# A searched instruction order with one load of V, half of the second weight's casts on VectorE, and a last output chunk in two column halves

## The chip, the cores and the metric

The kernel runs on one core of one Trainium2 chip. The metric is the device time of one execution in microseconds (us), median of several runs. The profile's span runs from the first to the last instruction and is 1.7 to 1.8 us shorter than the time of the same run (165.7 against 167.47 for the kernel before). Runs carry a state: a run more than 1.5% above the fastest of the same kernel in the same series is called slow and left out of comparisons. With few runs that label is coarse on one core; where it matters I give the granted clock (the share of TensorE's full clock that the chip allowed, mean over the span) beside it.

Engines: PE is TensorE, PEld its weight loads, DVE is VectorE, ACT is ScalarE, POOL is GpSimd, SP is SyncE, and a q after a name is the engine's instruction queue, where DMA issues are shown.

## The reference, cut to what matters

```python
# attention: gated linear recurrence, batch 4, 8 heads, 768 steps, head size 48
state = alpha[:, :, t, :, None] * state + einsum('bhd,bhe->bhde', k[:, :, t], v[:, :, t])
y[:, :, t] = einsum('bhd,bhde->bhe', q[:, :, t], state)
# mixer on x = y as (4, 768, 384)
u  = x + (x.T @ U @ V).T                   # low rank over the 768 steps: U 768x32, V 32x768
ch = maximum(u @ w_ch1, 0) @ w_ch2         # 384 -> 1536 -> 384
out = u + ch
```

The kernel computes the recurrence in chunks of 128 steps: six chunks for each batch, two at a time, called groups 0, 1 and 2.

## The kernel before

The program describes every operation to a small scheduler, `Plan`, with an engine, an assumed duration, a priority and its inputs. `Plan.run` replays these assumed times, decides in which order each engine gets its instructions, and only then emits them. The chip knows nothing of the assumed times: each engine works through its list in that order, and an instruction whose input is late holds up those behind it.

The places that the change and the argument touch, with cuts:

```python
# V is loaded four times, into four groups of 32 partitions
for g in range(4):
    P.add("POOL", 500, lambda g=g: nc.gpsimd.dma_start(vm_sb[32*g : 32*g+R, :], moe_V), ...)

# the two weights come in three pieces each; every piece is cast to bf16 in two halves
# (i < 3: first weight, i >= 3: second weight)
e = ((("POOL","POOL"),)+(("POOL","POOL"),)*2+(("POOL","POOL"),)*3)[i][hf]
...
op = P.add(e, cost[e], f_cast, r=[(t, i)], w=[...], prio=400 + i, port=True)

# attention, batch 0: which engine makes the products for groups 0, 1, 2
ek = ("DVE", "DVE", "POOL")[g] if first else "POOL"              # k times exp(-cum)
eq = ("DVE", "POOL", "POOL+DVE")[g] if first else (...)           # q times exp(cum)
parts = [(i, 1) for i in range(G)] if first and g in (2,) else [(0, G)]
...
for eng, dst, src, fac in ((ek, rk, kt, ai), (eq, rq, qt, aa)):
    for i0, n in parts if dst is rq else [(0, G)]:
        P.add(e, ..., f_mul(e, dst, src, fac, i0, n), ..., port=True)

# first MLP product: 12 blocks, evicted in turn by ScalarE and VectorE
if jt % 2 == 0:
    P.add("ACT", 500, ... Relu ..., w=[(h1, jt)], prio=100)
else:
    P.add("DVE", 560, ... tensor_scalar_max ..., w=[(h1, jt)], prio=100)

# second MLP product of a chunk: 12 matmuls, one sum on VectorE, one store
P.add("DVE", 550, lambda: nc.vector.tensor_tensor(ou(), xb()[:, c, :], hb()[:, 0, 0:DM], op=ALU.add), ...)
P.add("SP", 550, lambda: nc.sync.dma_start(out[b, c*C:(c+1)*C, :], ou()), ...)
```

The "first stage" below is batch 0's attention, from the start to the first MLP matmul. The "middle" runs from there to the sum of the last chunk but one; the "tail" is the rest.

## Time and profile before

| kernel before | us |
|---|---|
| median of the first three runs (range) | 167.73 (167.64 to 170.92) |
| profile: span | 165.7 |
| first MLP matmul | 31.23 |
| start of the sum of the last chunk but one | 160.37 |

The page's lines and the table of stretches are in the prediction. Two places, of which it has the numbers but not the lines: here they are from the timeline of the kernel before (start, duration, engine, source line, operation, out<-in, count, and in brackets the idle time before it with what ended it). First the first stage:

```profile
15.04 1.64 POOL L448 TENSOR_TENSOR rk<-io,ai 128x768 bf16<-128x768 f32 x1 [5.79 <-ACT ai L441]
...
15.48 2.01 DVE L448 TENSOR_TENSOR rq<-io,aa 128x768 bf16<-128x768 f32 x1
```

VectorE began its product 0.44 us after GpSimd had begun one, and it took about twice as long as one alone (the prediction has the numbers). Then the arrival of the second weight:

```profile
41.65 1.60 POOL L322 CAST w_sb<-io 128x768 bf16<-128x768 f32 x2 [7.65 <-DMA io<-in_moe_w_ch_dram]
```

GpSimd stood 7.65 us before the second weight came in at 41.65. PE had no wait for GpSimd in those 7.65 us, so the wait cost nothing. The stretches around it, from the table by stretch (duration, then busy us and instructions of PE, PEld, DVE, ACT and POOL, granted clock, DMA share, GB/s):

```profile
36.00:40.00 4.00, 3.85 (x38) 2.38 (x37) 1.17 (x3) 3.98 (x7) 0.00 (x0) 1.00 1.07 338
40.00:44.00 4.00, 4.00 (x27) 2.39 (x26) 2.33 (x5) 3.39 (x9) 2.35 (x3) 1.00 1.06 400
44.00:50.00 6.00, 5.38 (x43) 3.25 (x42) 0.96 (x2) 4.69 (x8) 6.00 (x7) 1.00 1.08 326
```

PE works through the arrival at full clock.

### The profile page before, as it was taken

Reading aid. Unit: us, or ns where it says so; the run is one execution under the profiler, and the core shown is the slowest. Engines: PE = TensorE matmul, PEld = TensorE weight load, DVE = VectorE, ACT = ScalarE, POOL = GpSimd, SP = SyncE. Lnnn points to the kernel's source line nnn. Section 1 sums busy time; section 2 is a strip of 40 time slices with the busy share of each in tenths; the row PEclk is TensorE's granted clock in tenths of the full one; section 3 lists DMA queues with packets and bytes.
Section 4 is the critical chain, followed back from the end, with each engine's and each line's share of the span. In section 5 each row is a group of like instructions: output and inputs, shape, how many; then the busy total and the mean of one; then the engine's idle time right before and its main releaser. Section 6 shows DMA issues by size and latency. Waiting matters only on the chain.

```text
span 165.7 us, 3925 instructions
## 1 busy us (share of the span) xinstructions
PE 156.9 (95%) x1635; PEld 96.0 (58%) x1635; DVE 89.9 (54%) x142; ACT 82.5 (50%) x153; POOL 54.0 (33%) x59
## 2 busy tenths in 40 slices
PE   5999999999989999999998899999999999999991
PEld 1454666656556767556556656576656565656560
DVE  2008983553508528588446719996849524544421
ACT  3169277569881894994625575434441212422200
POOL 8923864620994650486002239600000000000000
PEclk9999999999999999999999999999999999999999
DMA  3999999999999999999986998999003713001112
GB/s 99 274 288 203 194 190 384 349 283 368 383 316 316 244 322 249 262 336 313 225 200 137 317 295 113 207 213 171 24 6 82 155 69 120 4 1 68 70 56 95
DMA packets 58851, 33.15 MB, mean 200 GB/s; under 512 B 31440, under 2 KB 57680, under 8 KB 58832
## 3 DMA queue, kind: packets, MB, share of 16 engines
q1 hardware_dynamic: 46992, 24.38, 56.2%
q10 hardware_dynamic: 10864, 8.26, 17.9%
q0 software_dynamic: 976, 0.25, 1.4%
q8 instruction: 13, 0.21, 0.5%
q14 instruction: 6, 0.05, 0.1%
HBM read 24.08 MB, written 4.72 MB: 174 GB/s over the span
## 4 chain that ended last, share of the span: by engine, by line
PE 67%; DMA 10%; SPq 8%; issue 7%; POOL 4%; DVE 1%; ACT 1%; ACTq 0%; POOLq 0%
PE ps L686 28%; PE ps L664 21%; SPq L376 7%; DMA io<-in_moe_w_ch_dram 6%; DMA io<-in_alpha_dram 4%; PE ps L567 2%; PE ps L488 2%; POOL rk L448 2%; PE ps L520 2%; POOL w_sb L322 2%; PE ps L459 2%; PE ps L693 1%; PE ps L633 1%; PE ps L562 1%; POOL io L373 1%
## 5 line engine op out<-in xcount | busy, mean ns | idle before, releaser
L686 PE MATMUL ps<-w_sb,h1t 128*128 128x384 bf16 x288 | 55.3, 326 | 0.0
L664 PE MATMUL ps<-uT,w_sb 128*128 128x384 bf16 x288 | 52.2, 326 | 0.3 <-ACT xb L583 0.3
L675 ACT ACTIVATE h1t<-ps 128x384 bf16<-128x384 f32 x48 | 23.7, 493 | 38.9 <-PE ps L664 38.1
L677 DVE TENSOR_SCALAR h1t<-ps 128x384 bf16<-128x384 f32 x48 | 26.6, 555 | 25.0 <-PE ps L664 22.0
L664 PEld LDWEIGHTS <-w_sb 128*128 128x128 bf16 x288 | 27.7, 98 | 17.9 <-issue 0.5
L686 PEld LDWEIGHTS <-h1t 128*128 128x128 bf16 x288 | 27.3, 98 | 16.9 <-issue 0.5
L498 DVE TENSOR_TENSOR pm<-ps,ut_ones 128x1024 bf16<-128x1024 f32 x18 | 21.5, 1219 | 6.4 <-PE ps L488 3.7
L695 DVE TENSOR_TENSOR ou<-xb,ps 128x384 f32<-128x384 bf16 x24 | 13.2, 552 | 20.9 <-PE ps L693 10.4
L448 POOL TENSOR_TENSOR rk<-io,ai 128x768 bf16<-128x768 f32 x10 | 17.1, 1719 | 18.6 <-ACT ai L441 17.7
L704 PE MATMUL ps<-ones,ident 128*128 128x512 bf16 x55 | 15.4, 422 | 1.9 <-DVE rk L277 1.9
L448 DVE TENSOR_TENSOR rq<-io,aa 128x768 bf16<-128x768 f32 (+1 forms) x11 | 13.1, 1200 | 1.1 <-ACT aa L442 1.1
L322 POOL CAST w_sb<-io 128x768 bf16<-128x768 f32 x12 | 9.5, 828 | 11.4 <-DMA io<-in_moe_w_ch_dram 11.4
L583 ACT CAST xb<-ps 128x768 bf16<-128x768 f32 (+1 forms) x15 | 10.0, 672 | 5.4 <-PE ps L567 4.2
L417 ACT ACTIVATE lt<-io 128x768 bf16<-128x768 f32 x12 | 9.8, 841 | 5.2 <-DMA io<-in_alpha_dram 3.9
L362 POOL TENSOR_SCALAR_AFFINE_SELECT pm<-pm 128x1024 bf16<-128x1024 bf16 x6 | 6.5, 1091 | 17.4 <-DVE pm L498 11.8
L441 ACT ACTIVATE ai<-ps 128x768 bf16<-128x768 f32 x12 | 9.9, 822 | 3.2 <-PE ps L428 1.9
L322 POOL CAST rv<-io 128x768 bf16<-128x768 f32 (+1 forms) x11 | 9.7, 906 | 3.7 <-DMA io<-in_v_dram 3.7
L704 PEld LDWEIGHTS <-ident 128*128 128x128 bf16 x55 | 5.6, 107 | 8.2 <-issue 2.5
L442 ACT ACTIVATE aa<-ps 128x768 bf16<-128x768 f32 x12 | 10.0, 830 | 0.0
L567 PE MATMUL ps<-rv,pm 128*128 128x48 bf16 x192 | 8.3, 184 | 1.2 <-DVE pm L498 1.1
L567 PEld LDWEIGHTS <-pm 128*128 128x128 bf16 x192 | 7.1, 96 | 3.6 <-DVE pm L498 1.6
L505 ACT CAST pm<-ps 128x1024 bf16<-128x1024 f32 x6 | 6.1, 1018 | 5.3 <-PE ps L488 5.3
(66 smaller groups left out, 141.8 us busy)
## 6 DMA issues: line engine op xcount, KB each, us to landing
io<-in_moe_w_ch_dram SPq DMA_DIRECT2D x6, 768.0 KB, 8.9
out_dram<-ou SPq DMA_DIRECT2D x24, 192.0 KB, 2.3
io<-in_q_dram SPq DMA_DIRECT2D x6, 192.0 KB, 4.2
io<-in_v_dram SPq DMA_DIRECT2D x6, 192.0 KB, 4.0
vm_sb<-in_moe_V_dram POOLq DMA_DIRECT2D x4, 48.0 KB, 6.0
kt<-rk SPq DMA_TRANSPOSE x6, 4.0
qt<-rq SPq DMA_TRANSPOSE x6, 3.2
io<-in_alpha_dram SPq DMA_DIRECT2D x4, 0.2 KB, 11.3
```

Of the source, the lines that this page charges most:

```text
L322: ENG[eng].tensor_copy(dst, src)
L376: op = P.add("SP", 950, lambda t=t, src=src, c=c: nc.sync.dma_start(t()[:, :, 0:D].rearrange("p (h c) d -> p c h d", c=NC)[:, c], src[0, : ...
L442: P.add("ACT", 815, lambda: nc.scalar.activation(aa(), cb()[:, :, 0:DM], AF.Exp), r=[cb], w=[aa], prio=pe)
L448: ENG[eng].tensor_tensor(dst()[:, i0 : i0 + n, :, 0:D], ch(src, i0, n), fac()[:, i0 : i0 + n].rearrange("t g (h d) -> t g h d", d=D), op=A ...
L498: nc.vector.tensor_tensor(pmi().rearrange("t two hp c -> t (two hp) c"), sc().rearrange("p two (hp c) -> p (two hp) c", c=C), maskc.to_bro ...
L567: nc.tensor.matmul(y2[:, par, p, :], lhsT=pm[i]()[:, par, p, :], rhs=rv()[:, i, 2 * p + par, :], start=s0, stop=s1, skip_group_check=True,)
L664: nc.tensor.matmul(hb()[:, 0, 0:TW], lhsT=w1_sb[:, ct, jt * 128 : (jt + 1) * 128], rhs=uT()[:, 3 * tt : 3 * tt + 3, ct, :], start=(ct == 0 ...
L675: P.add("ACT", 500, lambda jt=jt, hb=hb: nc.scalar.activation(h1()[:, jt, :], hb()[:, 0, 0:TW], AF.Relu), r=[hb], w=[(h1, jt)], prio=100)
L677: P.add("DVE", 560, lambda jt=jt, hb=hb: nc.vector.tensor_scalar_max(h1()[:, jt, :], hb()[:, 0, 0:TW], 0.0), r=[hb], w=[(h1, jt)], prio=100)
L686: nc.tensor.matmul(hb()[:, 0, 0:DM], lhsT=h1()[:, jt, (c % 3) * C : (c % 3 + 1) * C], rhs=w2_sb[:, jt, :], start=(jt == 0), stop=(jt == NJ ...
L695: P.add("DVE", 550, lambda: nc.vector.tensor_tensor(ou(), xb()[:, c, :], hb()[:, 0, 0:DM], op=ALU.add), r=[hb, (xb, c)], w=[ou], prio=100)
L704: P.fill_fn = lambda i: nc.tensor.matmul(ps[:, i, 0:512], lhsT=ident, rhs=fill_in, start=True, stop=True)
```

## The change

The intent: a new order found by searching over the scheduler's options, with the engines re-assigned to fit; fewer bytes loaded (V once instead of four times, and spread to the four groups of partitions by a matmul); VectorE shares the casts of the second weight, since GpSimd was the busier of the two there; and a shorter end, since the last chunk's sum and store are split in two.

```diff
-        for g in range(4):
-            P.add("POOL", 500, lambda g=g: nc.gpsimd.dma_start(vm_sb[32 * g : 32 * g + R, :], moe_V), ...)
+        P.add("POOL", 500, lambda: nc.gpsimd.dma_start(v16(), moe_V), ...)
+        for hf in range(2):
+            P.add("PE", mm(TW), ... matmul(tb, lhsT=rep4, rhs=v16()[:, hf*TW:(hf+1)*TW]) ...)
+            P.add("DVE", 550, ... copy("DVE", vm_sb[:, hf*TW:(hf+1)*TW], tb) ...)
 ...
-                e = (... +(("POOL","POOL"),)*3)[i][hf]
+                e = (... +(("POOL","DVE"),)*3)[i][hf]
 ...
-        ek = ("DVE", "DVE", "POOL")[g] if first else "POOL"
+        ek = ("DVE", "POOL", "POOL")[g] if first else "POOL"
-        eq = (...) if first else ("DVE" if b in (0,1,2,3) else "POOL")
+        eq = (...) if first else ("DVE" if b in (0,1,2) else "POOL")
-        split = ((1,), (0,), ())[g] if b in (0,1,2) else ()
+        split = ((1,), (0,), ())[g] if b in (0,1) else ()
-        parts = [(i, 1) for i in range(G)] if first and g in (2,) else [(0, G)]
+        parts = [(i, 1) for i in range(G)] if first and g in (0,1,2) else [(0, G)]
 ...  # evictions of kT, qT, v and the state in batch 0, banks, three output buffers for four,
 ...  # store slack 700 for 3000, the scheduler's booking of ScalarE's DMA issues
     def mlp2(b, xb, h1, c, utx):
+        last = b == B - 1 and c == NC - 1
+        for n, (m0, m1) in enumerate(((0, DM // 2), (DM // 2, DM)) if last else ((0, DM),)):
+            ... 12 matmuls, sum and store of columns m0:m1, the same priorities for both halves
```

## The prediction

> **What bounds the kernel now.** I read the page's busy times and slices first, then the chain of waits, then the per-stretch table of busy times, then the timeline at both ends. From the page (busy time, share of span, instructions; then 40 slices of 4.14 us):
>
> ```profile
> PE 156.9 (95%) x1635; PEld 96.0 (58%) x1635; DVE 89.9 (54%) x142; ACT 82.5 (50%) x153; POOL 54.0 (33%) x59
> ...
> PE   5999999999989999999998899999999999999991
> ...
> PEclk9999999999999999999999999999999999999999
> DMA  3999999999999999999986998999003713001112
> ...
> L704 PE MATMUL ps<-ones,ident 128*128 128x512 bf16 x55 | 15.4, 422 | 1.9 <-DVE rk L277 1.9
> ```
>
> PE is the engine to count, but 95% is not all work: line 704 is filler, 55 dummy matmuls that keep the array warm, and a matmul's "busy" includes its pipeline tail. So I counted matmuls by their pitch instead, taken from the merged rows of the chain of waits: 36 of the 384-column matmuls in 5.86 us is 0.163 us each, 8 of the 128-column transposes in 0.45 us is 0.056, 8 or 16 of the small attention ones are 0.020 to 0.028. With the counts of each line that gives about 135 us of real matmul pitch in the whole program, 11.9 us of filler (55 at 0.2155, that is 512/2.4 plus 2.5 ns), and, up to 162.3 us, where the last matmul's result is handed over, about 15 us in which PE has nothing: 1.9 at the start, 5.7 more before 31.2 us, 7.3 after. These pitches are rounded, so each remainder carries perhaps 1 us of error.
>
> The same table of stretches (duration, then busy us of each engine with instruction counts, clock, DMA share, GB/s) shows the three regimes:
>
> ```profile
> 0.00:31.20 31.20, 28.36 (x336) 16.25 (x337) 14.20 (x24) 16.96 (x29) 19.58 (x29) 1.00 0.96 243
> ...
> 45.00:60.00 15.00, 14.51 (x184) 9.83 (x185) 6.50 (x10) 10.05 (x14) 10.12 (x10) 1.00 1.05 294
> 60.00:86.00 26.00, 25.77 (x275) 16.09 (x274) 16.47 (x24) 17.29 (x35) 9.15 (x7) 1.00 1.09 274
> 86.00:97.00 11.00, 9.78 (x196) 6.48 (x195) 6.68 (x8) 5.90 (x11) 2.18 (x2) 1.00 0.90 237
> ...
> 120.00:162.30 42.30, 42.28 (x273) 25.02 (x269) 20.01 (x37) 10.04 (x20) 0.00 (x0) 1.00 0.22 66
> ```
>
> Until 31.2 us the first batch's attention runs behind its loads (DMA share about 1); all filler lies here, the last at 27.5 us, and the first MLP matmul starts at 31.23. From there PE is nearly full; by pitch the holes are about 1.5 us between 31 and 60, about 1 in 60 to 75, 2.4 in 86 to 97, about 1.5 in the rest. From 120 us on there is no hole at all, so nothing that shifts evictions there can help. Then the tail, from the timeline:
>
> ```profile
> 156.27 6.01 PE L686 MATMUL ps<-w_sb,h1t 128*128 128x384 bf16 x36
> ...
> 162.32 0.55 DVE L695 TENSOR_TENSOR ou<-xb,ps 128x384 f32<-128x384 bf16 x1 [1.40 <-PE ps L686]
> ...
> 162.90 0.33 SPq L697 DMA_DIRECT2D out_dram<-ou  x1
> ```
>
> After the last matmul: 0.55 of add, 0.33 of issue, landing 1.9 us after issue start (164.8), end at 165.7: 3.4 us that no PE saving touches. So time = start of MLP (31.2) + remaining pitch (123.8) + holes (7.3) + tail (3.4), and 2.0 us between the span, 165.7, and the median time, 167.73.
>
> **What the Trainium skill says.** "TensorE: Matmul & The Clock Gate", section "Back-to-back issue gap", gives N/2.4 + 2.5 ns: 162.5 ns for 384 columns. The trace agrees (163). For 192 columns that is 82.5 ns, an estimate from the page; weight loads don't bind there as the trace runs 128-column transposes, each with its own load, at 56 ns. "DMA: Bandwidth & Descriptors", section "Anatomy of one DMA", puts most of a small transfer in a fixed part of about 2 us and only the rest in bytes; the last store of 192 KB landed in 1.9 us, with some 0.6 us of engine activity seen, so halving its bytes can save 0.3 us at most. Its section "Issuing engines are not separate DMA queues" says loads from all queues share the 16 engines: so the dropped V loads help only by their bytes. "SBUF — State Buffer" says that VectorE with two SBUF inputs and GpSimd block one another; the trace agrees: a product on VectorE beside a GpSimd product at 15.5 us took 2.01 us, two others, alone, 1.83 together.
>
> **The change, part by part.**
>
> *One V load.* GpSimd issues V four times at 0.50 us each; three go, 1.5 us of GpSimd. But its next task, the copy that gates the q and v loads, then waited 0.41 us for alpha, so issue time is not on the path. 3 x 48 = 144 KB leave saturated engines; at the 225 GB/s of 10 to 20 us that is 0.64 us of transfer, part of it in the shadow of alpha, so the first batch's chunks may land 0.4 us earlier. Added: two matmuls of 384 columns (0.33 us of PE, in time now filled) and two VectorE copies of 0.55.
>
> *First batch's engines.* The second k product moves from VectorE (0.92) to GpSimd (about 1.64), which sat idle 5.8 us until 15.04: VectorE is free 0.9 us earlier. Halving products, casts and evictions by chunk in groups 0 and 1 lets each start when its own chunk lands, at some 0.1 us fixed cost per extra piece. Those pieces and the V copies hand part of the 0.9 back. The end of this stage hangs on the last v chunk (its cast ended at 26.0) and the 5.2 us of state, mask, output, low-rank and eviction after it, which the change hardly shortens. Start of MLP: 0.7 us earlier, 30.5.
>
> *Second weight's casts.* Three of six go from GpSimd (0.83) to VectorE (0.56). In 40 to 50 us GpSimd was busy 8.35 of 10, and PE waited 0.49 us at 46.52 for its k product, which had queued behind two casts. That wait should go: 0.5 us.
>
> *Batches 2 and 3.* For batch 2 the mask loses its ScalarE copy (1.02) plus GpSimd select (1.09) and gets one VectorE product (1.22), two times; these stand in the 86-to-97 hole, where PE waited 1.1 us for a mask and ScalarE lost 0.58 us to issuing a load; the new plan books that issue. Batch 3's q product moves to GpSimd, 3 x 0.95 off VectorE, which is busy 9.4 of 10 between 100 and 110. I give 1.2 of the 2.4. PE work itself is not reduced. Fewer banks for MLP (two kept for attention), the state product confined to two banks, earlier stores with three output buffers instead of four: no net worth I can read, perhaps 0.1 gained.
>
> *The tail.* 12 matmuls at 162.5 become 24 at 82.5: +0.03. Both halves carry the same priorities step by step, and a tie goes to the lower number, so I read the plan as alternating them: half one ends only 0.08 us before half two. Then VectorE does two adds of about 0.35 (the 192-element product at 88.9 took 0.34), the second ending some 0.6 us after the last matmul, against 0.55 before; the issue takes 0.33 and isn't blocked; the last transfer has half the bytes, -0.3. Net -0.25. Had the halves run one after the other it would be about -0.5.
>
> Sum: -0.7 - 0.5 - 1.2 - 0.1 - 0.25 = -2.75, from 167.73: 165.0.
>
> **Rivals.** (1) *The load stream is the bound until about 45 us.* DMA share is about 1 there, GpSimd waited 7.65 us until 41.65 for the second weight, and its loads stay behind the first and alpha. Then an earlier MLP start is given back as a wait for the second weight, and only the transfer saved (0.4), the later holes and the tail count: about 166.0. Against it: after 46 us the casts waited for GpSimd, not for DMA. (2) *VectorE becomes the wait.* It gains 1.1 (V), 1.7 (casts), 2.4 (batch 2 masks) and loses 0.9, 0.7 (one eviction to ScalarE) and 2.9: about +0.8 on 90 busy, so no bound on average; but a late mask or V copy in the first 31 us moves everything, and fewer banks can hold PE back: 167 to 168. (3) *The new order closes nearly all holes.* PE's floor is an MLP start at about 30, 123.8 of pitch, 3.1 of tail and 2.0: 159. With 3 us of holes left: 162. For it: the order was searched with a plan that books more of the hardware's delays. Against: only about half of the holes have a cause that a named edit removes.
>
> **Range and chances.** Middle 165.0; 162.8 if holes fall below 4 us, 167.4 if rival 1 and part of 2 hold. 2% faster is 164.4, a little below my middle: 0.38 for faster, 0.59 for within 2%, 0.03 for slower, as PE work does not grow and the most heavily loaded stretch after 120 us is untouched.
>
> **What would show it.** Right: first MLP matmul near 30.5; no PE wait on a GpSimd product near 46; PE hole in batch 2's attention about halved; the last two adds of 0.35 back to back, and 3.1 to 3.2 us from the last matmul's result to the end. Wrong: the start of MLP unmoved or later (first-batch step), a new PE wait on weight casts after 40 us (rival 1), holes where attention waits for banks or masks (rival 2), or holes after 31 us below 4 us (I was too timid).

## The result

The changed kernel is correct, and slower. In the first series five runs took 172.07, 172.59, 172.69, 172.77 and 176.71 us (the last one slow, at clock 0.961); the kernel before had a median of 167.82. The ratio of the fast runs is 1.0284, 95% interval 1.0253 to 1.0315. Ratios here are the mean time of one kernel's fast runs over the mean of the other's of the same rounds, so not quite the ratio of the medians that I quote. My 165.0 was off by 7.7 us, my range ended at 167.4, and I had given "slower" a chance of 0.03.

The first profile of the changed kernel fell in the slow run, so I don't explain from it. (Its loss looks different: its start is at 37.49 us, and VectorE doesn't wait for the second weight there.) A profile in a fast run came with the repeat called a1 below (time 172.3, granted clock 0.988); its lines answer to those of before. The page:

```profile
span 170.6 us, 3950 instructions
...
PE 159.0 (93%) x1647; PEld 97.4 (57%) x1647; DVE 93.0 (55%) x150; ACT 80.9 (47%) x151; POOL 54.8 (32%) x57
...
PE   5998999982999999999999999999999999999991
...
PEclk9999999999699999999999999999999999999999
```

PE's busy time is only 2 us more than before. The row of slices shows where the time went: a slice is 170.6/40 = 4.27 us, PE falls to 2 in the tenth slice (38.4 to 42.6 us), and the granted clock to 6 in the eleventh. The stretches show it beside the same ones of before:

```profile
36.00:40.00 4.00, 3.07 (x25) 1.75 (x24) 0.21 (x1) 4.00 (x8) 0.00 (x0) 1.00 1.06 322
40.00:44.00 4.00, 1.08 (x6) 0.61 (x6) 1.89 (x4) 0.33 (x2) 2.13 (x2) 0.94 1.05 384
44.00:50.00 6.00, 6.00 (x37) 3.36 (x36) 2.96 (x6) 3.56 (x10) 3.08 (x3) 0.76 0.86 250
```

In 40 to 44 us PE is busy 1.08 us of 4 where before it was busy all 4, and afterwards its clock is 0.76 where before it was 1.00. The timeline there says why:

```profile
41.84 0.56 DVE L328 CAST w_sb<-io 128x768 bf16<-128x768 f32 x1 [5.62 <-DMA io<-in_moe_w_ch_dram]
41.87 1.22 POOL L328 CAST w_sb<-io 128x768 bf16<-128x768 f32 x1 [8.21 <-DMA io<-in_moe_w_ch_dram]
42.31 1.02 DVE L688 TENSOR_SCALAR h1t<-ps 128x384 bf16<-128x384 f32 x2
42.92 2.49 PE L675 MATMUL ps<-uT,w_sb 128*128 128x384 bf16 x9 [3.38 <-DVE h1t L688]
```

Read it from the bottom. PE waited 3.38 us for VectorE's eviction of an MLP block (L688), because the bank that it needed was still full (a bank is one of the eight parts of the tile `ps`, to which PE writes its products). That eviction's own input was long there; it began at 42.31 because it stood behind VectorE's cast of the second weight, and the cast had waited 5.62 us for the weight's load. GpSimd's cast waited 8.21 us for the same load and harmed nobody, exactly as before. So the load's lateness is old (41.65 before, 41.84 now); what is new is that an engine with something urgent behind it waits for it.

To place the rest I use three landmarks of each profile:

| profile | first MLP matmul | middle | tail | span | state of that run |
|---|---|---|---|---|---|
| before | 31.23 | 129.14 | 5.3 | 165.7 | fast |
| changed (a1) | 32.20 | 132.85 | 5.5 | 170.6 | fast |
| difference | +0.97 | +3.71 | +0.2 | +4.9 | |

By an estimate from these lines, the middle's +3.7 fits the hole (3.4) plus the lower clock (0.06 of 4 us and 0.24 of 6 us, 1.7 together), less waits of before that no longer occur, about 1.4 by subtraction.

### The profile page after: what moved, and what is told of

Same layout as the page of the kernel before. It is cut to its first block, busy times and chain, and to the rows that moved or that the text cites. A ratio compares the mean times of both kernels' runs of the same rounds, so it can differ in the third digit from the quotient of the medians.

```text
span 175.0 us, 3950 instructions
## 1 busy us (share of the span) xinstructions
PE 162.5 (93%) x1647; PEld 99.7 (57%) x1647; DVE 93.7 (54%) x150; ACT 81.2 (46%) x151; POOL 54.7 (31%) x57
## 4 chain that ended last, share of the span: by engine, by line
PE 75%; DMA 12%; DVE 5%; POOL 4%; ACT 1%; issue 1%; DVEq 0%; POOLq 0%
PE ps L701 27%; PE ps L675 21%; DMA io<-in_k_dram 12%; PE ps L499 4%; PE ps L470 4%; PE ps L578 4%; PE ps L713 2%; PE ps L573 2%; DVE rq L459 2%; PE ps L531 2%; POOL rk L459 2%; DVE pm L509 1%; PE ps L708 1%; PE ps L644 1%; POOL io L389 1%
## 5 line engine op out<-in xcount | busy, mean ns | idle before, releaser
L701 PE MATMUL ps<-w_sb,h1t 128*128 128x384 bf16 (+1 forms) x300 | 55.4, 320 | 0.0
L688 DVE TENSOR_SCALAR h1t<-ps 128x384 bf16<-128x384 f32 x48 | 26.5, 556 | 30.1 <-PE ps L675 28.0
L459 POOL TENSOR_TENSOR rk<-io,ai 128x768 bf16<-128x768 f32 x11 | 19.1, 1741 | 47.4 <-ACT ai L452 25.7
L509 DVE TENSOR_TENSOR pm<-ps,ut_ones 128x1024 bf16<-128x1024 f32 x20 | 24.2, 1221 | 7.6 <-PE ps L499 6.8
L709 DVE TENSOR_TENSOR ou<-xb,ps 128x384 f32<-128x384 bf16 (+1 forms) x25 | 13.3, 535 | 17.7 <-PE ps L701 9.7
L459 DVE TENSOR_TENSOR rq<-io,aa 128x768 bf16<-128x768 f32 (+1 forms) x9 | 10.9, 1229 | 0.2
L499 PE MATMUL ps<-qt,kt 48*128 48x128 bf16 x192 | 9.0, 232 | 0.4 <-DVE pm L509 0.2
L328 POOL CAST w_sb<-io 128x768 bf16<-128x768 f32 x9 | 7.3, 841 | 5.5 <-DMA io<-in_moe_w_ch_dram 5.5
L326 ACT CAST st<-ps 128x192 bf16<-128x192 f32 x11 | 3.5, 320 | 11.7 <-PE ps L531 7.0
L470 PE MATMUL ps<-ident,rk 128*128 128x128 bf16 x48 | 5.2, 275 | 3.6 <-POOL rk L459 3.3
L326 ACT COPY kt<-ps 128x1024 bf16<-128x1024 bf16 x5 | 5.1, 1026 | 7.4 <-PE ps L470 7.4
```

Of the source, the lines that this page charges most:

```text
L328: ENG[eng].tensor_copy(dst, src)
L459: ENG[eng].tensor_tensor(dst()[:, i0 : i0 + n, :, 0:D], ch(src, i0, n), fac()[:, i0 : i0 + n].rearrange("t g (h d) -> t g h d", d=D), op=A ...
L470: nc.tensor.matmul(t[:, i * HP + p, :], lhsT=src()[:, i, 2 * p : 2 * p + 2, :].rearrange("t h w -> t (h w)"), rhs=ident, start=True, stop= ...
L499: nc.tensor.matmul(s2[:, par, p, :], lhsT=kT()[o : o + D, i, p, :], rhs=qT()[o : o + D, i, p, :], start=(p == 0), stop=(p == HP - 1),)
L509: nc.vector.tensor_tensor(pmi().rearrange("t two hp c -> t (two hp) c"), sc().rearrange("p two (hp c) -> p (two hp) c", c=C), maskc.to_bro ...
L688: P.add("DVE", 560, lambda jt=jt, hb=hb: nc.vector.tensor_scalar_max(h1()[:, jt, :], hb()[:, 0, 0:TW], 0.0), r=[hb], w=[(h1, jt)], prio=100)
```

## The experiments

All kernels below gave correct results. They ran on five chips; each is compared with the kernel before on its own chip. "Start" is the first MLP matmul in the profile.

### First series: is it the first stage?

The slow profile showed the first stage as the late part. Its cause there seemed to be VectorE's products of two SBUF operands beside GpSimd's. So the first theories were about that.

**a0** is the changed kernel again, on another chip.

> The changed kernel once more, to get a profile of an undisturbed run (the one taken first had a granted clock of 0.961 and is not comparable). Time 172.1 to 172.8. Theory of the port: even at a full clock the two half q products of the first group on VectorE take about 2.0 us each (0.55 alone) while GpSimd forms k products, and the first MLP matmul starts 3 to 6 us after the 31.2 us of the kernel before. Rival, the clock: the late start at 37.5 us came from half-speed matmuls between 18 and 29 us; with the clock at 1.0 the start would be within 1 us of 31.2, and the 4.5 us lost would lie after it.

Measured: 173.07, 174.36 and 173.76 us at clocks of 0.979 to 0.985, and 169.93 at 1.00; beside that one the first three count as slow, and no ratio is given. The start was 33.84, 2.6 us later than before's and so a little short of the 3 to 6 expected. This profile fell in one of the slow runs; k1_sp below is the same program in a fast one, and there too the start was 33.70 and the two halves took 3.93 us together. In the first stage (from the timeline of a0):

```profile
13.55 1.79 POOL L459 TENSOR_TENSOR rk<-io,ai 128x768 bf16<-128x768 f32 x1 [4.29 <-ACT ai L452]
...
13.75 2.00 DVE L459 TENSOR_TENSOR rq<-io,aa 128x384 bf16<-128x384 f32 x1
...
15.68 1.99 DVE L459 TENSOR_TENSOR rq<-io,aa 128x384 bf16<-128x384 f32 x1
```

GpSimd's k product began 0.2 us earlier, and each of VectorE's half-size q products, which had been whole in the kernel before, then took 2 us. Half the work, the same 2 us, and each half ends about 0.4 us after a product of GpSimd's (15.75 after 15.34): the time is mostly waiting for GpSimd's instruction to end, and splitting the product made VectorE pay it twice.

**one_q** joins the two halves of group 0's q product again.

```diff
+ if first and g == 0 and dst is rq:        # half 0 does nothing, half 1 does both chunks
+     fm = (lambda *a: None) if i0 == 0 else (lambda e, dst, src, fac, i0, n: f_mul(e, dst, src, fac, 0, 2))
```

> The order of all instructions kept; only the first group's q product on VectorE is one instruction for both chunks instead of two halves. Theory of the port (a VectorE product of two SBUF operands waits for a whole GpSimd product that began first, once per instruction): one wait instead of two, the product is done about 1.5 us earlier (near 16 us instead of 17.4), the MLP starts 1 to 2 us earlier, time 1 to 2 us less than the changed kernel, 170.5 to 171.5. Rival, late q chunks: the halves were long because of data, then the single product ends as late or later, and time is the same or up to 0.5 us more.

Measured: 172.39 us median, ratio 1.0244 (1.0183 to 1.0306). The product began before GpSimd's this time, took 0.96 us, and the start came 1.7 us earlier than in a0, at 32.10. So the product won the race instead of losing it once, which is not the test that was meant; w2_pool_one_q below lost it, and its single product took 2.03 us, against 3.9 for two halves. The time is above the expected 170.5 to 171.5 and gained nearly nothing: the middle was 133.31 us against a0's 131.89. PE waited 3.4 us behind the weight's cast instead of 3.1, although the weight landed at 41.19 and not at 42.57, and the clock behind the wait was lower (0.59 in 40 to 45 us). The earlier start was given back there, part of it to the clock.

**rk_dve** takes GpSimd out of the first stage's k products altogether.

```diff
+ if first and dst is rk:
+     fm = lambda e, *a: f_mul("DVE", *a)
```

> The order of all instructions kept; the first batch's three k products all run on VectorE at their place in its order, so that no GpSimd product runs beside the q halves. Theory of the port: each half takes about 0.55 us, the second is done by 15.5 to 16 us, MLP starts 2 to 4 us earlier than in the changed kernel, time 169 to 170.5. Rival, VectorE's sum of work: three more or less serial products of 0.92 us delay the q halves as much as the port did; the time stays within 0.7 us of the changed kernel. Rival, late q chunks: halves stay near 2 us.

Measured: 176.67 us, ratio 1.0525 (1.0449 to 1.06), start 36.82: a clear miss. GpSimd, without its k product, went on to its q halves at once and ran into VectorE's, as the timeline has it:

```profile
15.19 0.92 POOL L459 TENSOR_TENSOR rq<-io,aa 128x384 bf16<-128x384 f32 x1 [5.74 <-ACT tot L455]
...
15.25 1.27 DVE L459 TENSOR_TENSOR rq<-io,aa 128x384 bf16<-128x384 f32 x1
```

VectorE began 0.06 us later and took 1.27 us instead of 0.55. Moving one partner of a collision away had moved the next one in, and VectorE had one product more to do. This kernel differs too much from the changed one to measure the collision by it.

**k1_sp** issues batch 1's k load from SyncE's queue instead of ScalarE's, so that it queues behind the second weight.

```diff
- nc.scalar.dma_start(t()[:, :, 0:D], src[b]...)
+ (nc.sync if (b, n) == (1, 1) else nc.scalar).dma_start(t()[:, :, 0:D], src[b]...)
```

> The order of all instructions kept; the second batch's k load is issued by SyncE at its place in the order (ahead of the later second-weight loads and of q) instead of by ScalarE, whose queue reached it late, at 37 us. Theory of the late load: k lands before 45 us instead of 50, the PE hole of about 3 us in front of the second batch's k transposes at 50 to 54 us shrinks to under 1, the start of MLP stays where it is, time 2 to 3 us less than the changed kernel, 169.5 to 170.5. Rival, weight casts: the hole moves to the second weight, whose loads now land later, and the time stays within 0.7 us.

Measured: 171.36 us, ratio 1.0187 (1.0109 to 1.0265). The start was 33.70, as in a0; VectorE waited 3.6 us instead of 4.7 for the weight, PE 2.0 instead of 3.1, and the middle was 130.85 against 131.89. The trace shows the load still issued on ScalarE's queue, at 33.20, where a0 has 33.35. The function that issues is called after the loop has ended, when `n` is 3, so the condition was never true, and a comparison of the two programs shows the same instructions on every engine. So this is a failed edit and the changed kernel once more. As a second sample it is useful: with the same program the weight landed at 41.32 instead of 42.57, and the hole was 1.1 us shorter. The idea itself stays untested.

### Second series: the casts, and the tail alone

**w2_pool** gives all casts back to GpSimd and changes nothing else; the order stays.

```diff
  def f_cast(dst=dst, stage=stage, e=e, hf=hf, i=i):
+     e = "POOL"
```

> The changed kernel's order kept; its three second-weight casts on VectorE run on GpSimd at their place. Theory of the blocked queue: VectorE, which works through its list in order, stood 4.7 us before a cast whose load had not landed, with the MLP's evictions behind it, so PE stood 3.1 us; with the casts on GpSimd the hole at 40 to 44 us goes, the clock stays at 1.0, and the time falls by 3 to 5 us to 167 to 169.5. Rival, the load stream itself: PE waits for the second weight anyway and stands as long a little later; the time falls by less than 1 us. Rival, the first-stage slip is the whole loss: less than 1 us too.

Measured: 168.2 us, four runs from 167.81 to 168.59 at clocks of 0.995 to 1.0, ratio 0.999 (0.9931 to 1.0049). The whole loss is gone. The hole is too, in the table by stretch:

```profile
40.00:44.00 4.00, 4.00 (x34) 2.50 (x32) 2.06 (x4) 3.07 (x10) 2.63 (x3) 1.00 1.06 394
44.00:50.00 6.00, 4.82 (x40) 2.95 (x39) 1.18 (x4) 3.62 (x5) 5.25 (x6) 1.00 1.08 318
```

PE is busy all of 40 to 44 us, at clock 1.00; after 44 it has a smaller hole, 1.2 us, where it waits for GpSimd's k product, queued behind the casts. That is the wait, 0.49 us in the kernel before, that I had meant the moved casts to remove, and in gate_only and a1, with casts on VectorE, no such wait shows. So moving the casts saves a wait of about one us and makes one of two to more than three.

There was a catch: in this profile the first stage had also gone well. From its timeline:

```profile
13.69 0.55 DVE L460 TENSOR_TENSOR rq<-io,aa 128x384 bf16<-128x384 f32 x1
...
14.33 1.89 POOL L460 TENSOR_TENSOR rk<-io,ai 128x768 bf16<-128x768 f32 x1 [5.32 <-ACT ai L453]
```

VectorE began first, its half took 0.55 us, and the start was 32.17. The instruction order of this stage is the same in a0 and here; which of the two begins first hangs on a few tenths of a us.

**w2_pool_one_q** is w2_pool with one_q's edit.

> The casts on GpSimd as in w2_pool, and the first group's q product in one piece as in one_q. If both causes are real and the first one's gain was hidden behind the blocked VectorE (one_q alone started the MLP 1.7 us earlier, yet gained nothing clear), it is now seen: 1 to 2 us below w2_pool, 165.5 to 168. If the load stream bounds this stage, no gain over w2_pool.

Measured: 168.82 us, ratio 1.0033 (0.9974 to 1.0093). In this profile GpSimd began first, the single product took 2.03 us, and the start was 32.72. The expected gain over w2_pool did not come. But against one_q this is the cleanest pair for the casts: the first stage's edits are the same, the start is even 0.6 us later, and the ratio falls from 1.0244 to 1.0033, because the middle shrinks from 133.31 to 128.60 us.

**b_w2_dve** makes the reverse: the kernel before, with every second cast of the second weight on VectorE.

```diff
+ e = "DVE" if i >= 3 and hf == 1 else "POOL"
```

> The kernel before with its order kept, and every second cast of the second weight on VectorE in place of GpSimd: this part of the change alone. Theory of the blocked queue: a VectorE wait of several us for the weight's load, a PE hole of 2 to 4 us near 40 us, a clock below 1.0 after it in some runs, time 170 to 172. My prediction's reading (GpSimd relieved): 0 to 0.5 us faster than before.

Measured: 168.9 us, ratio 1.0012 (0.9944 to 1.0081) over its four fast runs, 168.38 to 169.15. The profiled run is the fifth: 171.28 us at clock 0.989, called slow. It shows the hole; from its list of waits (engine, what waits and for what: us in all, times, longest):

```profile
DVE w_sb L322 <- DMA io<-in_moe_w_ch_dram: 4.1, 1, 4.1
...
PE ps L665 <- DVE h1t L678: 2.7, 1, 2.7
```

So the mechanism came, and the time of the other four runs did not. I can't see into those four: a weight that landed a little earlier there would explain it, and so would a PE that had more to do before it needed the bank. The order differs too, and so do the banks: the diff leaves the MLP of batches 0 to 2 six banks of the kernel before's eight, and no run has that part alone (in w2_pool six banks do no harm by themselves). That stays open. The time missed its expected 170 to 172, and what the run says is that the cast on VectorE is not harmful in every order.

**b_tail** is the kernel before with only the last chunk's two halves.

> The kernel before with only the last chunk's second product, sum and store in two column halves. Prediction: the halves' matmuls alternate on PE, the two adds of about 0.35 us follow each other, the last store has half the bytes: 0.25 us less than before (0 to 0.5). Rival: the second store waits for the first on the queue or lands as late as the undivided one, no gain.

Measured: 169.79 us, ratio 1.0069 (1.0011 to 1.0127). The start in this profile was 32.39 against 31.23, though nothing before 155 us was changed, so the time holds chance in the first stage as well. And it holds the clock, as this page's row shows:

```profile
PEclk9999999999999999999999599999999999999999
```

Slice 23 lies at 92.6 to 96.8 us, in code that is the kernel before's. So the tail has to be read by itself, from the start of the sum of the last chunk but one to the span's end: 5.8 us against 5.3. The gain didn't come; the rival expectation held.

### Third series: which cast, which race, which tail

**w2_first** gives back only the cast that waits, the second weight's first piece; the other two stay on VectorE.

```diff
  def f_cast(...):
+     e = "POOL" if i == 3 else e
```

> The changed kernel's order kept; of the three second-weight casts on VectorE only the first, the one that waited 4.7 us for its load, runs on GpSimd. Theory of the blocked queue: the wait for the load, not the casts, was the harm; the PE hole at 40 to 44 us is gone as in w2_pool, VectorE waits for no weight load, and the time is that of w2_pool, 167.5 to 168.5, or up to 0.7 us less as GpSimd keeps less work ahead of the k products. Rival: the VectorE work of the casts is the harm; then most of the loss stays, 170 or more.

Measured: 170.39 us, ratio 1.0103 (1.0039 to 1.0166); the profile is of a slow run (175.4 us, clock 0.977). VectorE has no wait for the first piece there. It lost the race in the first stage (13.64 against GpSimd's 13.28; halves of 2.00 and 1.99 us), and batch 1's k load landed late, at 46.9, with a hole of its own before the k product. A slow run is not to be explained by, so I keep only the ratio. By it most of the loss is gone with one cast; but the median lies outside the expected 167.5 to 168.5 and just in the rival's range, so this run alone doesn't part the wait from the casts' work.

**w2_first_seq** lets the last chunk's halves run one after the other as well.

```diff
- ... w=[hb], prio=pr + g)
+ ... w=[hb], prio=pr + g + 12 * n)
```

> w2_first, and the last chunk's two halves one after the other on PE instead of alternating. Theory of the tail: the first half's sum and store pass while the second half is multiplied; after the last matmul one sum of 0.35 us instead of two that end 0.62 us after; 0.2 to 0.4 us less than w2_first. Rival: the end of the program is set by the landing of whichever store was issued last plus a fixed part; still 0.2 us less. No gain would mean that neither sum nor store size counts.

Measured: 168.55 us (three fast runs, and one slow of 175.61), ratio 1.0008 (0.995 to 1.0066), start 32.24; VectorE began first, 13.77 against 14.40, with halves of 0.55. The tail took 5.2 us. The median is 1.8 us less than w2_first's, more than a tail can explain, so w2_first holds a loss that I can't name. But two of the three casts are on VectorE here too, VectorE doesn't wait for the weight's first piece, and the loss is gone: that speaks for the wait, and against the casts' work, as what cost.

**w2_first_gate_seq** makes the outcome of the race certain: GpSimd first reads a few columns of VectorE's second q half, and so begins its second k product after it.

```diff
+ nc.gpsimd.tensor_copy(seen, dst()[:, 1, 0, 0:8])      # after VectorE's second half
+ for a in late_k: f_mul1[0](*a)                         # then the k product
```

> w2_first_seq, and GpSimd's k product of the second group waits until VectorE has formed both q halves of the first group (GpSimd first reads eight columns of the second half). Theory of the port: both halves take 0.55 us in every run instead of 0.55 or 2.0 by who begins first; MLP starts at 32 to 32.7 us in the profile, the runs spread less (within 1 us) with the clock at 1.0; time 167 to 168. Rival: GpSimd's later k product now holds up the second group and the start of MLP is as late as with the port lost, 33.5 us or more, time 168.5 to 169.5.

Measured: 168.9 us, six runs from 168.34 to 169.79, ratio 1.0037 (0.9994 to 1.0081). The gate does its work, in the timeline:

```profile
13.07 1.02 DVE L462 TENSOR_TENSOR rq<-io,aa 128x384 bf16<-128x384 f32 x2
...
14.15 0.19 POOL L474 COPY seen<-rq 128x8 bf16<-128x8 bf16 x1 [4.86 <-DVE rq L462]
```

Both halves together took 1.02 us, and the start was 31.90. The time is above the expected 167 to 168 and in the rival's range, though the start was not late as the rival had it. It is no faster than w2_first_seq, which had won the race by chance in its profile.

**b_tail_seq** is b_tail with halves one after the other.

> The kernel before with the last chunk in two column halves, one after the other on PE. In the profile, from the start of the last but one sum to the end of the span: 5.3 us in the kernel before, 5.8 with alternating halves; here 5.0 to 5.2. Time within 0.3 us of the kernel before, which is below what its runs scatter. Rival: splitting costs whatever the order, 5.5 us or more.

Measured: 169.57 us, ratio 1.0052 (0.9992 to 1.0113), start 33.42, tail 5.4 us, between the two expectations; the clock fell in slice 23 as in b_tail. With b_tail and b_w2_dve this makes four profiles of the first stage of the kernel before, unchanged: 31.06, 31.23, 32.39 and 33.42. That kernel has such races too, and its start varies by over 2 us; but who wins doesn't settle its start, as VectorE's product won in b_tail (0.95 us) and the start was later than with the 2.01 above.

### Fourth series: the late stages, and the best sum

**b_late** puts some of the later batches' part of the change into the kernel before: batch 3's q product on GpSimd, the state product in two banks, the earlier stores, the new booking of ScalarE's issues.

> The kernel before with only parts of the change that act after 45 us (batch 3's q product on GpSimd, the state product confined to two banks, earlier stores, the plan's booking of ScalarE's load issue); casts, V loads, first batch and the undivided tail as before. Theory that the loss lies in the first 45 us alone and the later edits are worth what I predicted for them (1.2 us): 1 to 1.6 us less than before, MLP start as before at 31 to 32.5. Rival, given back: the hole at 86 to 97 us shrinks and holes after 100 us grow as in w2_pool, time within 0.5 us of before.

Measured: 168.07 us, ratio 1.0009 (0.9953 to 1.0066); the profile fell in a slow run.

**b_late2** is another cut of it: batch 3's q product, the second weight's load earlier in the queue, earlier stores, three output buffers, the booking, no allowance for the transposes.

> As b_late by another set of the change's later edits (three output buffers, transposes trusted earlier, the second weight's loads ahead, instead of the state product's banks). Same expectations: 1 to 1.6 us less than before if later edits hold on the chip, within 0.5 us if they are given back.

Measured: 168.08 us, ratio 1.0005 (0.995 to 1.006). Neither moves the time, with intervals of some 0.6% either way; a gain of 1.2 us would be 0.7%, outside both. But neither has the edit of batch 2's mask (`split`), which carried much of the 1.2 in the prediction, so they don't test that part.

**w2_pool_gate_whole** is the sum of what had helped: all casts on GpSimd, the gate, and the last chunk undivided.

> The changed kernel with both faults of its first 45 us mended (all second-weight casts on GpSimd, GpSimd's k product after the two q halves) and the last chunk undivided. If those two and the tail are the whole loss: clock at 1.0 and spread under 1.5 us, 166.5 to 168, at or below the kernel before. If something else of the change costs as well: 168.5 or more.

Measured: 168.44 us, ratio 1.0038 (0.9995 to 1.0081), all six runs between 168.29 and 169.02 at clocks of 0.996 or more. The steadiest version, and not a faster one; it fell between the two expectations. No version that I ran beats the kernel before.

### Fifth series: the two causes taken apart

In w2_pool both causes were gone at once, since its profile had won the race. So the changed kernel was run with only the race mended, casts left as they were (**gate_only**), beside the changed kernel itself (**a1**).

> The changed kernel with only the gate on GpSimd's second k product of the first stage; all three casts of the second weight stay on VectorE, the tail stays in alternating halves. Theory A (the casts in VectorE's queue are the main cause, whatever the port did): MLP starts at 31.9 to 32.3 us, VectorE still waits 3 to 5 us for the second weight, PE's hole in 40 to 45 us is 2 us or more, and the ratio to the kernel before is 1.012 to 1.025. Theory B (the lost port is the root: it delays ScalarE's issue of batch 1's k load from 31.7 to 33.3 us, and the late loads make the hole): the k load is issued by 31.8 us, PE's hole is under 1 us, and the ratio is 0.998 to 1.008.

> The changed kernel once more, as the companion on the same chip. Both theories: first VectorE half of q at 2.0 us if GpSimd's k product started first, MLP start 33.5 us or later in that case, ratio 1.02 to 1.03 over its fast runs. If the profile happens to show the half at 0.55 us and yet a hole of 2 us or more in 40 to 45 us, theory A gains; if it shows the half at 0.55 us, no hole and about 168 us, theory B gains.

Measured: gate_only 171.89 us, ratio 1.0261 (1.0197 to 1.0324); a1 172.16 us, ratio 1.0206 (1.0142 to 1.027). Mending the race alone gains nothing. In gate_only's profile (fast, clock 0.989) both halves took 1.02 us together, batch 1's k load was issued at 31.47 and the start was 31.97, all as they should be, and still its timeline has:

```profile
40.99 0.56 DVE L328 CAST w_sb<-io 128x768 bf16<-128x768 f32 x1 [5.01 <-DMA io<-in_moe_w_ch_dram]
...
42.07 2.11 PE L689 MATMUL ps<-uT,w_sb 128*128 128x384 bf16 x9 [3.40 <-DVE h1t L702]
```

VectorE waited 5.01 us for the weight, and PE 3.40 for VectorE. Theory A, the casts, stands, a little above the top of its range; theory B, the race as the root, falls. Beside it, w2_pool_gate_whole has the same gate with all casts on GpSimd (and the undivided tail, 0.2 us), and its ratio is 1.0038 against 1.0261: with the race taken out of both, the casts cost 2.2%, or 3.7 us. a1's start was 32.20, earlier than the 33.5 that a lost race was expected to give: VectorE had begun its first half 0.2 us before GpSimd, and lost only the second half to it (2.00 us at 13.90).

a1 also shows what the clock adds: its runs at a granted clock of 1.00 took 170.31 and 170.44 us, those at 0.986 to 0.988 took 172.02 to 172.32. (In the first series, though, a run at 1.00 took 172.07, so the clock isn't all that differs between runs.)

The landmarks of the profiles, side by side:

| profile | casts on VectorE | start | middle | tail | span |
|---|---|---|---|---|---|
| before | none | 31.23 | 129.14 | 5.3 | 165.7 |
| w2_pool | none | 32.17 | 128.63 | 5.5 | 166.3 |
| w2_pool_one_q | none | 32.72 | 128.60 | 5.6 | 166.9 |
| w2_pool_gate_whole | none | 31.95 | 129.55 | 5.3 | 166.8 |
| w2_first_seq | not the first | 32.24 | 129.67 | 5.2 | 167.1 |
| w2_first_gate_seq | not the first | 31.90 | 129.76 | 5.2 | 166.9 |
| b_tail | none | 32.39 | 130.23 | 5.8 | 168.4 |
| k1_sp (= changed) | all three | 33.70 | 130.85 | 5.5 | 170.1 |
| gate_only | all three | 31.97 | 132.23 | 5.5 | 169.7 |
| a1 | all three | 32.20 | 132.85 | 5.5 | 170.6 |
| one_q | all three | 32.10 | 133.31 | 5.5 | 170.9 |

All of these are fast runs. The middle is 128.6 to 129.8 us where VectorE does not wait for the weight (130.2 in b_tail, where the clock fell), and 130.9 to 133.3 where it does. In the second group the latest start has the shortest middle, as the weight's landing, and not the start, sets when PE goes on: from the landing (the start of VectorE's cast) to the end of the middle k1_sp, gate_only and a1 take 123.2 us each, with starts 1.7 us apart (one_q, with the lowest clock, 124.2). In the first group it is 118.7 to 120.1 from the start of the first cast.

## Why the prediction was wrong, by its own steps

**Second weight's casts: the step that failed.** I had -0.5 us. Between one_q and w2_pool_one_q, the pair with the same first-stage edits, the same term is 3.6 us of the median (172.39 against 168.82) in the other direction. I had counted the casts by throughput: GpSimd was busy 8.35 of 10 us in 40 to 50, VectorE had room, so share the work. I had the number that mattered in the same text, the wait of 7.65 us until 41.65 for this weight, and used it only in rival 1, as a bound on PE's progress. I never asked which queue would do that waiting after the change, and what else stood in it. VectorE has an MLP eviction about every us there (41.55, 42.52, 43.50, 44.47 in w2_pool), and PE has only as much to do ahead as there are free banks: in a1 VectorE began to wait at 36.22, and PE ran dry at 39.54, 3.3 us later. I wrote "a new PE wait on weight casts after 40 us" as a sign of rival 1; the sign came, but by another road: PE waited not for the weight but for an unrelated eviction behind the cast.

The hole then cost more than its length, as the clock fell behind it (0.76 in 44 to 50 us). The Trainium skill, "TensorE: Matmul & The Clock Gate", section "HAM oscillation — how this bites in real kernels", warns of idle gaps of PE above about 3.4 us. Here waits of 3.4 us (a1) and also of 2.0 us (k1_sp, clock 0.84 in 40 to 45 and 0.82 in 45 to 50 us) and 2.7 us (b_w2_dve) went with a lower clock; w2_pool and before, without such a hole, show 1.00. This is no threshold: b_tail, b_tail_seq and before all have the same wait of 1.07 us for a mask (near 92 us), and it was followed by a clock of 0.50 for about 3 us in the first two and by 1.00 in before. So whether the clock falls behind a short hole is partly chance. I had priced no hole at more than its length.

**First batch's engines and one V load: not reached, and lost in chance.** I had the start of MLP at 30.5, from one profile of 31.23. The fast profiles of the changed kernel have 32.20 and 33.70, its variants at best 31.90; the first stage of before, unchanged, has 31.06 to 33.42 in four profiles. A gain of 0.7 could not have been read from one profile of each. The V load's part fits its size, but isn't shown: the first k product began at 12.2 to 13.0 us in the profiles with one load, against 13.14 before (12.8 to 14.5 in its variants, so the two overlap). I did not run it alone. What I missed is the race. The Trainium skill, "SBUF — State Buffer", section "Who interferes with whom", says that the order of issue decides who is blocked, for the whole instruction. The runs agree: 0.55 us for the half that began first, 2.0 for the one that began second. I had quoted the 2.01 us of the product before and gone on to charge "some 0.1 us fixed cost per extra piece". Splitting a product that loses the race made it lose twice (3.9 us for two halves, 2.03 for one piece). Yet gate_only shows that this is not what made the kernel slow: with the race mended the loss stayed.

**Batches 2 and 3: the holes shrank, the time did not.** I gave 1.2 us of the hole in 86 to 97. The hole did shrink. This is the table by stretch for the kernel before:

```profile
86.00:100.00 14.00, 12.78 (x222) 8.32 (x221) 7.28 (x10) 8.68 (x17) 3.82 (x4) 1.00 0.86 236
```

And the same stretch of w2_pool, which has this part of the change and no hole at the weight:

```profile
86.00:100.00 14.00, 13.46 (x222) 8.54 (x219) 9.84 (x12) 6.65 (x14) 4.83 (x3) 1.00 1.00 246
```

PE is busy 0.7 us more of these 14 us. From 60 us to the end of the middle PE is idle 0.53 us in w2_pool against 1.78 before: 1.25 less, much as forecast, though it is one profile each and the mask's edit was not run alone. But w2_pool's whole middle is only 0.5 us shorter than before's. Between the start and 60 us PE is idle 0.40 us more, with the waits for GpSimd's k product, and it is busy 0.33 us more in the whole middle; then the start was 0.9 us later.

**The tail: the form right, the gain absent.** I had read the halves as alternating, and they do: two sums back to back in 0.62 us. I had -0.25 us. Measured from the sum of the last chunk but one, the tail is 5.5 us in w2_pool and a1 and 5.8 in b_tail, against 5.3 before. From w2_pool's timeline:

```profile
162.70 0.62 DVE L710 TENSOR_TENSOR ou<-xb,ps 128x192 f32<-128x192 bf16 x2 [1.34 <-PE ps L702]
163.08 0.81 SPq L711 DMA_DIRECT2D out_dram<-ou  x2
```

What I left out is the second issue. The two stores leave one queue one after the other, 0.81 us for both against 0.33 for the one before, and that can eat what the smaller transfer saves: 96 KB landed in 1.6 to 1.7 us, 192 KB in 1.9. (The section "Anatomy of one DMA", which I had drawn on, describes DMAs issued by GpSimd; these stores are SyncE's, and the traces' durations count.) One after the other the tail is 5.2 us in w2_first_seq and w2_first_gate_seq and 5.4 in b_tail_seq: no clear gain where I had said 0.5.

**The rivals.** Rival 1 was half right: an earlier start is given back at the second weight, as k1_sp and gate_only show (123.2 us from the landing on in both). But I took this wait as a ceiling on the gain, not as a source of loss. Rival 2 named VectorE as the wait, and looked for it in busy sums and in the first 31 us; VectorE was not too busy, it stood still. Rival 3 did not come.

**In sum.** Without the casts' term, my other terms come to -2.25 us; w2_pool, the changed kernel without it, is at 0.999 of before. So the other terms together came out near nothing (its interval is 0.6%, or 1 us, either way), and the term with the wrong sign carried the result. A chance of 0.03 for "slower" was far too small for a change that re-orders four in-order queues; that no work was added was no argument against a wait.

Two slips of the working change nothing: 512/2.4 + 2.5 is 215.8 ns and not 215.5, and the 2.0 us between span and time compares two runs; the profiled run itself took 167.47, so 1.8.

**What stays open.** Why the same cast cost b_w2_dve's fast runs nothing; what w2_first lost; how the loss divides between the hole itself and the clock behind it (a1's two levels, 1.8 us apart, suggest that a good third is clock, and one run in the first series speaks against reading it so simply); and what the first stage's edits are worth in the mean of many runs, as a profile shows a single one.

## What to carry to other kernels

Before moving an operation to another engine, ask what it waits for and what stands behind it in the new queue: a wait that was free on an idle engine can cost several us on an engine that frees another's buffers (here 2 to 3.4 us of PE, and the clock behind it), however much busy time that engine has to spare. An engine's share of busy time says nothing of this; the idle time in brackets before the operation, in the kernel before, shows the wait. And split an instruction that shares a port with another engine only if you have made sure which of the two begins first.

## What the Trainium skill lacked or had wrong

- "SBUF — State Buffer": its rule on who is blocked is right here. What it lacks is how narrow the race is and what splitting does: with the same instruction order in that stage, VectorE began 0.6 us before GpSimd in one profile and 0.2 us after it in another, and each half-size product then took 0.55 or 2.0 us.
- "TensorE: Matmul & The Clock Gate": it puts the idle gap that lowers the clock at about 3.4 us. Here gaps in PE of 2.0 and 2.7 us were followed by mean clocks of about 0.8 over the next 5 to 6 us as well, and one of 1.07 us by 0.50 for about 3 us in two profiles (b_tail, b_tail_seq), but not in before.
- "DMA: Bandwidth & Descriptors": splitting the last store into two of 96 KB on one queue cost 0.81 us of issue against 0.33, and each landed in 1.6 to 1.7 us against 1.9 for 192 KB; the two sections named in the prediction give no figure for the further issue.
- None of the pages that I used prices an in-order engine's wait by what stands behind it: here a cast that waited 5.6 us held up an eviction, and PE for 3.4 us.
